# Dispatch scores of a soft mixture of experts taken straight from the tokens in four column groups, with another order of issue

## Chip, cores and metric

One core of a Trainium2 chip runs the whole program. The metric is device time in microseconds (us) of one execution; lower is better. The engines are named as in the profile: PE is TensorE's matmul side and PEld its weight loads, DVE is VectorE, ACT is ScalarE, POOL is GpSimd, SP is the engine that issues all DMAs here.

## What is computed

Windowed attention with four sink tokens, then a soft mixture of experts on its output. Cut to what matters:

```
B, H, S, D = 4, 8, 768, 64        # n_sink = 4, window = 128
a = softmax(q @ k.T / 8, masked to sinks and the last 128 positions)
x = (a @ v), heads side by side                 # 3072 tokens x 512
logits = x @ phi                                # 3072 x 32 slots
d = softmax(logits, over all tokens)            # dispatch
slot_input = d.T @ x                            # 32 x 512, 4 slots for each of 8 experts
slot_out[e] = relu(slot_input[e] @ w1[e]) @ w2[e]
c = softmax(logits, over the 32 slots)          # combine
out = c @ slot_out                              # 3072 x 512
```

## The kernel before

**Jobs.** The 3072 tokens are cut into 12 jobs of 256 tokens (4 batches of 3). For each job PE transposes K and Q (`prep`), multiplies scores in quarters of its array (`softmax.scores`, four steps of 8 matmuls, on PSUM tiles called s), DVE masks and takes maxima, ACT takes exponentials, POOL multiplies by the inverse sums, PE transposes the weights (`weights_transposed`), DVE or ACT copies them out, POOL cuts them into two masked copies (`select`), PE multiplies by the values in column halves (`values`, two steps of 2 and 8 or 12 matmuls), and the result lands in `xt`, 128 rows (two heads each of which there are four groups `a`) by 256 tokens. `natural` transposes it back to tokens by features (`xnb`).

**Tokens.** `Moe.tokens` (line 306) keeps a running softmax over all tokens of the dispatch. Scores are wanted twice, as [32 g + slot, token] for four groups g: groups 0 and 1 raw, groups 2 and 3 with the exponential, and the even groups hold the job's first 128 tokens, the odd ones the last. Before, this took three steps: `pairs` (line 328) multiplies phi's four chunks by xt's four chunks, each in a column group of its own, 256 tokens wide; a copy of 128x256 brings the four partial sums out of PSUM (line 334, on DVE or ACT); `logits` (line 337) adds the four up with a 0/1 matrix `c.slot`, once for each group g, 128 tokens wide. Then DVE takes the maximum (line 355) and its running minimum of negatives (358), ACT copies the raw half to `lt` (360), takes the exponential of the other half (362) and the factor for older sums (368), PE transposes `lt` (372), and `products` (384) multiplies it with `xnb`, four column groups again.

**Which order.** A planner (`Plan`) issues every step of the jobs. Each step has a key, 4.0 times the job's number plus an offset from the table `CFG`; the planner walks a modelled time and takes, of the steps that are ready on an engine, the one with the smallest key. All results of the planner are fixed before launch: each engine runs its list in order and waits on semaphores. PE works in four shapes: the whole array (transposes), quarters (scores), halves (values), column groups of 32 (`pairs`, `logits`, `products`). PSUM has two s tiles of two banks and four w banks; a w bank is needed by each of the transposes, values and token steps, until the copy out of it is done.

**Ends.** After the last job `finish` (418) turns the sums into slot inputs, `tail` (530) runs the experts' two layers on streamed weights and writes the output. Nothing in `tail` is touched.

Of the kernel before, what the change touches and what calls it, by code (L numbers as in the profile page):

```python
# [8 lines left out]
F32 = mybir.dt.float32  # L9
# [10 lines left out]
P = 128  # L20
# [257 lines left out]
class Moe:  # L278
# [6 lines left out]
    def __init__(self, nc, c, keep, work, pools, B):  # L285
        self.nc, self.c, self.keep, self.work, self.pools, self.B = nc, c, keep, work, pools, B

        self.lt = keep.tile([P, P], F32, name="lt")
        self.lb = keep.tile([P, 2, 2, 32], F32, name="lb")
        self.spare = keep.tile([P, 256], F32, name="spare")  # L290
# [12 lines left out]
        nc.gpsimd.memset(self.eps[64:96], EPS)  # L303
        nc.vector.memset(self.z, 0.0)

    def tokens(self, plan, keys, b, j, x, xn, blocks):
# [17 lines left out]
        if both:  # L324

            A, lp = plan.psum(), self.lp
# [16 lines left out]
        else:  # L343
            next(k), next(k)

            def logits(e):
                for a in range(4):
                    for g in range(4):
                        nc.tensor.matmul(L["tile"][32 * g:32 * g + 32, 0:P], lhsT=c.phi[:, a, :],
                                         rhs=xt[:, a, x[blocks[0]]], start=(a == 0), stop=(a == 3))  # L350

            plan.add(next(k), "P", 1.2, logits, r=xs + ["phi"], w=[L["name"]], new=L)

# [64 lines left out]
    def finish(self, plan, keys):  # L418
# [10 lines left out]

        swap, slots, sel = self.si.rearrange("p k s -> p (k s)"), self.spare[:, 0:P], self.sel  # L430
# [7 lines left out]
        plan.add(next(k), "V", 0.6, selectors, w=["fsel"])  # L438
        mm = [("m", 0), ("m", 1)]
# [8 lines left out]
        def inputs(e):  # L448
            for x in range(2):
# [8 lines left out]
            rz, self.z, f, self.eps, op0=ALU.mult, op1=ALU.add), r=["z", "f"], w=["rz"])  # L458
        plan.add(next(k), "V", 0.2, lambda e: nc.vector.tensor_copy(
            slots.rearrange("p (g s) -> p g s", g=4), c.slot.unsqueeze(1).to_broadcast([P, 4, 32])), w=["lp"])  # L460
        plan.add(next(k), "P", 0.25, lambda e: nc.tensor.matmul(Z["tile"][:, 0:1], lhsT=slots, rhs=rz, start=True, stop=True),
                 r=["rz", "lp"], w=["fz"], new=Z)
        plan.add(next(k), "V", 0.17, lambda e: nc.vector.reciprocal(rz, Z["tile"][:, 0:1]), r=["fz"], w=["rz"], last=Z)
# [153 lines left out]
class Weights:  # L617
# [9 lines left out]
    def load(self, t):  # L627
# [5 lines left out]
        else:  # L633
# [8 lines left out]
PT = 3  # L642
CFG = {'prep': [-2.17, -0.88],
       'load': [-3.57, -6.02],
       'v': [-0.18, -0.24],
       'S': -8.73,
       'M': 36.62,
       'E': -5.46,
       'N': 0.31,
       'K0': 2.19,  # L650
       'T': [3.66, 4.85, 4.7, 5.73],
       'K': -1.8,
       'sel': [-6.52, -2.35, 5.2, 5.48],
       'val': [3.28, -5.83, 5.91, 8.36],
       'xn': [2.08, 9.26],
       'tok': [7.72, -14.81, -29.67, 6.11, -4.29, -10.76, 19.93, 9.29, -24.99, 9.79, 6.46, -0.14, -1.55],
       'sm': -17.55,
       'sinks': -36.55,
       'tr': [83.54, 111.89, 84.43, 86.17, 89.04, 123.77, 106.32, 93.21, 89.01, 82.18, 84.62, 87.83, 68.6, 87.87, 106.87,
              85.72, 98.54, 75.2, 46.43, 23.9, 60.71, 53.42, 48.6, 43.21, 70.53, 50.67, 57.49],  # L660
       'w': [14.83, 8.0],
       'fin': [-17.88, 7.56, 0.7, -0.3, 12.51, 20.97, 18.11, 14.38, 20.61, 23.73, 38.59],
       'xn1': [18.28, 18.07],
       'tok1': [4.6, -7.87, -9.73, -4.24, 1.2, -17.1, 3.61, 11.52, -24.18, -0.27, -3.93, 3.34, -6.83]}


def window_path(ctx, tc, c, moe, q, k, v, phi, w1, w2, out):
# [21 lines left out]
    xt = moe.xt = u[:, 1024:2048].rearrange("p (a y) -> p a y", a=4)  # L689
    moe.lp = moe.spare[:, 0:256]  # L690

# [207 lines left out]
    def values(keys, n, quad):  # L899
# [20 lines left out]

        r = [("xw", quad, i, 1) for i in range(2)] + [("xw", quad, 1, 0, x) for x in range(2)]
        r += [("vb", 2 * n % 4), ("vb", (2 * n + 1) % 4), "vsink", "pst"]
        if j > 0:
            r += [("xw", quad, 0, 0, x) for x in range(2)] + [("vb", (2 * n - 1) % 4)]
        add(keys[0], "P", 2.15 if j else 1.72, go, r=r, w=[h["name"]], new=h, mode=HALVES)
# [17 lines left out]
    O = CFG  # L943
# [77 lines left out]
def general_path(ctx, tc, c, moe, ints, q, k, v, phi, w1, w2, out):  # L1021
# [87 lines left out]
    t, u = moe.first  # L1109
    moe.lp, xnb = t[:, 0:256], (u[:, 0:512], u[:, 512:1024])  # L1110
    moe.xt = u[:, 1024:2048].rearrange("p (a y) -> p a y", a=4)
    gate(nc, plan, c, phi, moe.acc[:, 0:P], "acc")
    for b in range(B):
# [10 lines left out]
        moe.slot_softmax(plan, 0, b, ())  # L1124
    moe.finish(plan, [0] * 11)
    moe.place(slot(), [0, 1], 2)
# [100 lines left out]
```

## Time and profile before

| | |
|---|---|
| median of 3 runs | 257.99 us (257.02 to 258.0) |
| profiled execution | 257.78 us, its span 256.0 us |
| mean granted clock of TensorE | 0.964 |
| busy: PE, DVE, ACT, POOL | 229.0, 171.2, 143.6, 141.3 us |
| jobs, until the slot inputs stand | up to about 201 us |
| experts and output | about 201 to 256 us |

A share of busy time is an average over the whole span. PE's time is read best from the starts of its steps in the timeline, since the ends of matmuls are modelled and overlap the next step: the distance between two starts is what the step costs.

### The profile page before, as it was taken

How to read it: one execution, taken by the hardware profiler on the slowest of the kernel's cores; microseconds unless marked ns; L12 is line 12 of the kernel's file. 1: busy time of each engine (PE TensorE's matmuls, PEld its weight loads, DVE VectorE, ACT ScalarE, POOL GpSimd, SP SyncE). 2: the span in 40 equal slices, each digit the busy share in tenths (PEclk: the TensorE clock that was granted, in tenths of full speed). 3: DMA queues.
4: the chain of work that ended last, by engine and by line, in shares of the span. 5: the costliest groups of instructions: out<-in, count | busy, mean ns of one | idle time of the engine just before them, and what ended most of it. 6: DMA issues, size and time to landing. Idle time of an engine off the chain costs nothing.

```text
span 256.0 us, 7069 instructions
## 1 busy us (share of the span) xinstructions
PE 229.0 (89%) x2572; PEld 157.2 (61%) x2572; DVE 171.2 (67%) x457; ACT 143.6 (56%) x568; POOL 141.3 (55%) x281
## 2 busy tenths in 40 slices
PE   7778999999999999999999999999699999997800
PEld 7655766776777776676777667677367434345700
DVE  3378968889798979979897997987514513103800
ACT  2367677568596757769675767977615112103700
POOL 1146769587685958669595857869964060000000
PEclk9979999999999999999999999999979999999955
DMA  5699869789899989967999866240609899950995
GB/s 126 133 176 225 227 152 356 186 239 379 162 257 211 343 250 302 276 146 244 256 366 223 235 125 123 59 150 4 206 13 358 300 399 422 414 235 0 399 394 203
DMA packets 84494, 59.34 MB, mean 232 GB/s; under 512 B 76261, under 2 KB 76261, under 8 KB 82917
## 3 DMA queue, kind: packets, MB, share of 16 engines
q1 hardware_dynamic: 84452, 58.83, 76.4%
q8 instruction: 22, 0.36, 0.6%
q14 instruction: 20, 0.16, 0.2%
HBM read 52.53 MB, written 6.29 MB: 230 GB/s over the span
## 4 chain that ended last, share of the span: by engine, by line
PE 66%; DVE 16%; ACT 6%; POOL 5%; issue 3%; ACTq 0%; POOLq 0%; DVEq 0%
PE w L127 47%; PE s L127 17%; DVE wt L127 7%; POOL wt L127 4%; DVE s L127 4%; ACT wt L127 3%; PE w L1179 1%; ACT wt L613 1%; DVE sums L127 1%; DVE first L127 1%; DVE pst L127 1%; DVE spare L127 1%; DVE qt L127 0%; DVE wt L599 0%; ACT wt L598 0%
## 5 line engine op out<-in xcount | busy, mean ns | idle before, releaser
L127 POOL TENSOR_TENSOR wt<-wt 128x528 f32<-128x528 f32 (+1 forms) x96 | 64.3, 673 | 36.3 <-DVE wt L127 22.1
L127 ACT ACTIVATE wt<-s,wt 128x132 f32<-128x132 f32 x192 | 68.8, 386 | 5.6 <-DVE wt L127 5.0
L127 POOL TENSOR_SCALAR_AFFINE_SELECT wt<-wt 128x512 f32<-128x512 f32 x88 | 54.0, 638 | 6.9 <-ACT wt L127 6.4
L127 PE MATMUL w<-wt 128*64 128x128 f32 (+3 forms) x550 | 51.7, 322 | 2.1 <-DVE wt L599 1.5
L127 PE MATMUL s<-wt,qt 64*64 64x196 f32 (+2 forms) x768 | 41.8, 327 | 4.5 <-ACT wt L127 3.7
L127 PEld LDWEIGHTS w<-wt 128*64 128x64 f32 (+2 forms) x550 | 36.7, 143 | 14.8 <-DVE wt L599 2.2
L127 PE MATMUL w<-ident,first 128*128 128x128 f32 x288 | 42.3, 279 | 1.7 <-ACT call L127 1.4
L127 ACT ACTIVATION_READ_ACCUMULATOR wt<-s,wt 128x1 f32 x192 | 42.5, 221 | 0.0
L127 PE MATMUL w<-ident,wt 128*128 128x128 f32 x250 | 38.3, 281 | 1.2 <-POOL wt L127 0.6
L127 PEld LDWEIGHTS w<-ident,first 128*128 128x128 f32 x288 | 32.5, 142 | 7.3 <-issue 2.3
L127 PEld LDWEIGHTS s<-wt,qt 64*64 64x64 f32 x768 | 26.5, 134 | 14.5 <-issue 6.5
L127 DVE TENSOR_REDUCE wt<-s 128x4 f32<-128x528 f32 x48 | 33.9, 707 | 1.7
L127 PEld LDWEIGHTS w<-ident,wt 128*128 128x128 f32 x250 | 28.1, 146 | 11.2 <-issue 3.4
L127 ACT COPY first<-w 128x512 f32<-128x512 f32 x28 | 16.5, 588 | 30.3 <-PE w L127 30.2
L127 ACT COPY wt<-w 128x512 f32<-128x512 f32 x36 | 21.1, 594 | 17.5 <-PE w L127 14.9
L127 DVE COPY_PREDICATED s<-later,s 128x256 f32<-128x256 uint8 x48 | 20.4, 424 | 8.9 <-PE s L127 8.0
L127 DVE COPY wt<-w 128x512 f32<-128x512 f32 x36 | 24.3, 677 | 1.5 <-PE w L127 0.8
L127 DVE COPY first<-w 128x512 f32<-128x512 f32 x20 | 13.7, 684 | 2.0 <-PE w L127 1.9
L127 PE MATMUL w<-wt,si 128*32 128x512 f32 x128 | 13.9, 593 | 0.4 <-DVE si L127 0.4
L127 PE MATMUL s<-wt 128*32 128x512 f32 (+1 forms) x144 | 14.3, 498 | 0.0
L127 DVE MEMSET s<- 64x512 f32 (+1 forms) x16 | 6.2, 385 | 9.5 <-PE s L127 9.1
L127 DVE TENSOR_TENSOR wt<-wt 128x4 f32<-128x4 f32 x48 | 11.2, 232 | 1.8 <-POOL wt L127 0.9
(120 smaller groups left out, 243.9 us busy)
## 6 DMA issues: line engine op xcount, KB each, us to landing
wt<-in_moe_w_dram SPq DMA_DIRECT2D x30, 1024.0 KB, 7.6
wt<-in_v_dram SPq DMA_DIRECT2D x24, 256.0 KB, 3.3
first<-in_q_dram SPq DMA_DIRECT2D x22, 256.0 KB, 3.8
first<-in_k_dram SPq DMA_DIRECT2D x22, 256.0 KB, 4.5
out_dram<-wt SPq DMA_DIRECT2D x5, 1024.0 KB, 5.6
first<-in_moe_w_dram SPq DMA_DIRECT2D x2, 1024.0 KB
out_dram<-wt SPq DMA_DIRECT2D x2, 512.0 KB
first<-in_k_dram SPq DMA_DIRECT2D x4, 128.0 KB, 3.0
```

The lines of the kernel that those rows point to most:

```text
L127: return self.tc.keep_in_program_order(f(*args, **kw))
L613: (nc.vector.tensor_copy if i else nc.scalar.copy)(ob[:, n - n0, i], yp)
L1179: nc.tensor.matmul(t[:, 0:P], lhsT=c.ident, rhs=c.ident, start=True, stop=True)
```

## The change

`tokens` loses `pairs`, the copy and the sum with `c.slot`. The new `logits` multiplies each of the four chunks of phi by the same chunk of xt for every group g, 16 matmuls of 128 tokens in four column groups, and adds the chunks up in PSUM. One w bank and one step on DVE or ACT go with it. `finish` makes its 0/1 matrix `slots` early, with the other selectors. `tied` changes nothing, as `CFG` has no entry `tie`. Every number of `CFG` is another one, and with them the order on all engines.

```diff
-            def pairs(e):
-                for a in range(4):
-                    nc.tensor.matmul(A["tile"][32 * a:32 * a + 32, 0:256], lhsT=c.phi[:, a, :], rhs=xt[:, a, :],
-                                     start=True, stop=True)
-            plan.add(next(k), "P", 0.45, pairs, r=xs + ["phi"], w=[A["name"]], new=A, mode=(128, 32))
-            plan.add(next(k), "AV", (0.27, 0.34), lambda e: (nc.scalar.copy if e == "A" else nc.vector.tensor_copy)(
-                lp, A["tile"][:, 0:256]), r=[A["name"]], w=["lp"], last=A)
-            def logits(e):
-                for g in range(4):
-                    nc.tensor.matmul(L["tile"][32 * g:32 * g + 32, 0:P], lhsT=c.slot, rhs=lp[:, x[g % 2]],
-                                     start=True, stop=True)
-            plan.add(next(k), "P", 0.23, logits, r=["lp"], w=[L["name"]], new=L, mode=(128, 32))
+        def logits(e):
+            for a in range(4):
                 for g in range(4):
+                    nc.tensor.matmul(L["tile"][32 * g:32 * g + 32, 0:P], lhsT=c.phi[:, a, :],
+                                     rhs=xt[:, a, x[g % 2 if both else blocks[0]]], start=(a == 0), stop=(a == 3),
+                                     skip_group_check=True)
+        plan.add(next(k), "P", 0.87, logits, r=xs + ["phi"], w=[L["name"]], new=L, mode=(128, 32))
...
+            nc.vector.tensor_copy(slots.rearrange("p (g s) -> p g s", g=4),
+                                  c.slot.unsqueeze(1).to_broadcast([P, 4, 32]))
...
-       'S': -8.73,
-       'M': 36.62,
+       'S': -57.08,
+       'M': 186.71,
...
```

The order on PE, one job in the middle, before. `s<-wt,qt` is a score step, `w<-ident,...` are transposes (first_76 is K or Q, first_77 the job's result, wt the weights), `phi` is `pairs`, `spare,slot` the sum over heads, `lb` the products, `pst,vsink` and the 64-row matmuls the values:

```order
L127 MATMUL w<-ident,wt 128x128 x4
L127 MATMUL w<-first_77,lb 32x256 x4
L127 MATMUL s<-wt,qt 64x196 x8
...
L127 MATMUL w<-ident,first_77 128x128 x4
L127 MATMUL w<-first_77,phi 32x256 x4
L127 MATMUL w<-ident,wt 128x128 x4
L127 MATMUL w<-ident,first_76 128x128 x4
L127 MATMUL w<-spare,slot 32x128 x4
L127 MATMUL s<-wt,qt 64x196 x16
```

and the same place now:

```order
L127 MATMUL w<-ident,wt 128x128 x2
L127 MATMUL s<-wt,qt 64x196 x8
L127 MATMUL w<-first_77,phi 32x128 x16
L127 MATMUL w<-first_77,lb 32x256 x4
L127 MATMUL s<-wt,qt 64x196 x8
L127 MATMUL w<-ident,first_77 128x128 x8
L127 MATMUL w<-ident,first_76 128x128 x4
L127 MATMUL w<-ident,wt 128x128 x4
L127 MATMUL w<-ident,first_76 128x128 x8
```

Three visits to the column groups have become one, the new scores stand right ahead of the products of the job before, and the transposes stand together. Counted over one job, PE changed its shape 13 times before and does so 9 times now; over the whole program 169 and 123 times.

The end of the jobs on PE, from the scores of the last job but one to the transpose of `lt` that waits for them, before:

```order
L127 MATMUL w<-first_77,phi 32x256 x4
L127 MATMUL w<-ident,wt 128x128 x4
L127 MATMUL w<-ident,qt 128x128 x2
L127 MATMUL w<-spare,slot 32x128 x4
L127 MATMUL w<-ident,lt 128x128
```

and now:

```order
L127 MATMUL w<-first_77,phi 32x128 x16
L127 MATMUL w<-ident,wt 128x128 x2
L127 MATMUL w<-ident,first_77 128x128 x8
L127 MATMUL w<-ident,wt 128x128 x4
L127 MATMUL w<-ident,lt 128x128
```

Fourteen transposes now stand between the finished scores and the transpose that waits for them, where none stood.

ACT, the token steps of a job in the middle, before:

```order
L127 COPY lt<-w 64x128
L127 ACTIVATE lt,sums<-w,sums 64x128
L127 COPY wt<-w 128x4x128
L127 ACTIVATE sums<-sums 128x1
L127 ACTIVATE wt<-s,wt 128x132 x4
L127 COPY lb<-w 128x64
```

and now:

```order
L127 COPY lt<-w 64x128
L127 COPY wt<-w 128x4x128
L127 ACTIVATE lt,sums<-w,sums 64x128
L127 COPY first_77<-w 128x512
L127 ACTIVATE sums<-sums 128x1
L127 COPY wt<-w 128x4x128
```

`COPY wt<-w 128x4x128` empties a bank of transposed K, `COPY first_77<-w` one of the transposed result. Three such copies now stand among the token steps, and PE's next transposes need the banks.

## Rows read from the trace of the kernel before

**Rows 1.** Stretches: window, length, then PE, PEld, DVE, ACT, POOL busy (count), granted clock.

```profile
62.00:78.00 16.00, 16.00 (x193) 11.33 (x195) 14.09 (x37) 12.38 (x52) 12.33 (x24) 1.00 0.91 227
...
174.00:190.00 16.00, 13.74 (x140) 9.13 (x138) 8.31 (x20) 8.88 (x35) 14.76 (x33) 0.89 0.25 84
```

**Rows 2.** Timeline of PE, 164 to 184 us: start, length, line, operation, count of records.

```profile
165.24 1.52 PE L127 MATMUL w<-wt 128*64 128x256 f32 x16
166.69 1.56 PE L127 MATMUL s<-wt,qt 64*64 64x196 f32 x32
168.18 0.65 PE L127 MATMUL w<-ident,first 128*128 128x128 f32 x4
...
170.30 0.64 PE L127 MATMUL w<-first,phi 128*32 128x256 f32 x8
170.87 0.66 PE L127 MATMUL w<-ident,wt 128*128 128x128 f32 x4
171.45 0.90 PE L127 MATMUL s<-wt,qt 64*64 64x196 f32 x16
172.28 0.43 PE L127 MATMUL w<-spare,slot 128*32 128x128 f32 x8
172.63 0.50 PE L127 MATMUL w<-pst,vsink 128*128 128x256 f32 x2
173.06 1.96 PE L127 MATMUL w<-wt 128*64 128x256 f32 x24
174.95 0.90 PE L127 MATMUL s<-wt,qt 64*64 64x196 f32 x16
...
179.05 0.64 PE L127 MATMUL w<-first,lb 128*32 128x256 f32 x8
179.62 0.44 PE L127 MATMUL w<-ident,qt 128*128 128x128 f32 x2
```

**Rows 3.** Chain that ended last, in order of time: the first job of two batches.

```profile
61.33 1.77 PE w L127 x16
...
105.02 1.77 PE w L127 x16
```

**Rows 4.** Groups by form: weight loads of `pairs`; busy us, mean ns, idle before.

```profile
L127 PEld LDWEIGHTS w<-first,phi 128*32 128x32 f32 x96 | 1.9, 108 | 2.1 <-issue 1.0 <-ACT wt L127 0.5 <-ACT first L127 0.3
```

**Rows 5.** Groups by form, DVE: maxima, whole-bank copy, masking, copy behind `pairs`.

```profile
L127 DVE TENSOR_REDUCE wt<-s 128x4 f32<-128x528 f32 x48 | 33.9, 707 | 1.7
L127 DVE COPY wt<-w 128x512 f32<-128x512 f32 x36 | 24.3, 677 | 1.5 <-PE w L127 0.8
L127 DVE COPY_PREDICATED s<-later,s 128x256 f32<-128x256 uint8 x48 | 20.4, 424 | 8.9 <-PE s L127 8.0
L127 DVE COPY spare<-w 128x256 f32<-128x256 f32 x10 | 4.1, 413 | 0.0
```

**Rows 6.** Groups by form, POOL: masked copies, products with inverse sums.

```profile
L127 POOL TENSOR_SCALAR_AFFINE_SELECT wt<-wt 128x512 f32<-128x512 f32 x88 | 54.0, 638 | 6.9 <-ACT wt L127 6.4 <-DVE wt L127 0.3
L127 POOL TENSOR_TENSOR wt<-wt 128x528 f32<-128x528 f32 x48 | 52.5, 1094 | 32.4 <-DVE wt L127 22.1 <-PE w L127 5.6 <-ACT wt L127 4.3
```

**Rows 7.** Timeline of all engines, 183 to 191 us, the token steps of job 10.

```profile
183.16 0.43 PE L127 MATMUL w<-spare,slot 128*32 128x128 f32 x8
...
184.03 0.60 DVE L127 TENSOR_TENSOR sums<-sums 128x1 f32<-128x1 f32 x1
...
184.99 0.36 ACT L127 ACTIVATE lt<-w,sums 64x128 f32<-64x128 f32 x1
...
185.49 0.33 PE L127 MATMUL w<-ident,lt 128*128 128x128 f32 x1 [1.91 <-ACT lt L127]
...
187.65 2.99 PE L127 MATMUL w<-wt 128*64 128x256 f32 x24
...
190.57 0.51 PE L127 MATMUL w<-pst,vsink 128*128 128x256 f32 x2
```

**Rows 8.** Stretch of 5 us behind that wait; columns as in the first group.

```profile
186.00:191.00 5.00, 4.92 (x37) 3.08 (x36) 0.91 (x2) 0.49 (x3) 3.55 (x9) 0.66 0.01 3
```

More of the change, by code (lines that the diff above doesn't have):

```diff
@@ L289, in __init__ @@
         self.lb = keep.tile([P, 2, 2, 32], F32, name="lb")
-        self.spare = keep.tile([P, 256], F32, name="spare")
+        self.spare = keep.tile([P, P], F32, name="spare")
         self.sel = keep.tile([P, 2, 32], F32, name="sel")
@@ L427, in finish @@
         sf = self.lt[:, 0:64].rearrange("p (h s) -> p h s", h=2)
-        swap, slots, sel = self.si.rearrange("p k s -> p (k s)"), self.spare[:, 0:P], self.sel
+        swap, slots, sel = self.si.rearrange("p k s -> p (k s)"), self.spare, self.sel
         def selectors(e):
@@ L435, in selectors @@
                 nc.vector.tensor_copy(sv[:, :, i], iv[:, :, 1 - i])
+            nc.vector.tensor_copy(slots.rearrange("p (g s) -> p g s", g=4),
+                                  c.slot.unsqueeze(1).to_broadcast([P, 4, 32]))
             nc.vector.reduce_sum(sel, c.ident.rearrange("p (h i s) -> p h s i", h=2, i=2), axis=AX.X)
-        plan.add(next(k), "V", 0.6, selectors, w=["fsel"])
+        plan.add(next(k), "V", 0.8, selectors, w=["fsel"])
         mm = [("m", 0), ("m", 1)]
@@ L458, in finish @@
             rz, self.z, f, self.eps, op0=ALU.mult, op1=ALU.add), r=["z", "f"], w=["rz"])
-        plan.add(next(k), "V", 0.2, lambda e: nc.vector.tensor_copy(
-            slots.rearrange("p (g s) -> p g s", g=4), c.slot.unsqueeze(1).to_broadcast([P, 4, 32])), w=["lp"])
         plan.add(next(k), "P", 0.25, lambda e: nc.tensor.matmul(Z["tile"][:, 0:1], lhsT=slots, rhs=rz, start=True, stop=True),
-                 r=["rz", "lp"], w=["fz"], new=Z)
+                 r=["rz", "fsel"], w=["fz"], new=Z)
         plan.add(next(k), "V", 0.17, lambda e: nc.vector.reciprocal(rz, Z["tile"][:, 0:1]), r=["fz"], w=["rz"], last=Z)
@@ L642 @@
 PT = 3
-CFG = {'prep': [-2.17, -0.88],
-       'load': [-3.57, -6.02],
-       'v': [-0.18, -0.24],
-       'S': -8.73,
-       'M': 36.62,
[L648 to L664, printed above, removed]
+CFG = {'prep': [-2.16, -0.3],
+       'load': [21.99, 22.32],
+       'v': [33.66, 32.25],
+       'S': -57.08,
+       'M': 186.71,
+       'E': 198.38,
+       'N': -122.03,
+       'K0': -153.45,
+       'T': [4.22, 5.36, -56.02, 6.26],
+       'K': -91.54,
+       'sel': [-252.14, -110.82, -227.04, -165.5],
+       'val': [6.47, -181.65, 159.49, 3.35],
+       'xn': [-3.88, -28.66],
+       'tok': [-94.42, -47.32, -0.46, -84.53, 6.22,
+               13.54, -86.04, -42.65, 121.57, 82.4,
+               -4.36],
+       'sm': -36.24,
+       'sinks': -8.72,
+       'tr': [243.6, 70.64, 138.55, 13.83, 356.42,
+              165.29, 138.6, 311.63, 323.87, 66.49,
+              76.22, 267.84, 70.54, 249.06, 174.54,
+              11.97, 188.69, 179.1, -43.61, -32.41,
+              114.32, 92.2, -113.6, 355.77, 23.25,
+              3.05, 157.35],
+       'w': [43.54, 8.0],
+       'fin': [142.31, 142.48, 171.48, 3.97, -103.29,
+               142.9, 61.71, 69.87, -120.32, 16.75],
+       'xn1': [-22.56, -92.79],
+       'tok1': [-164.89, 33.0, -16.85, 236.68, -3.11,
+                1.53, -78.29, -119.18, 63.7, 47.24,
+                44.44]}
 def window_path(ctx, tc, c, moe, q, k, v, phi, w1, w2, out):
@@ L689, in window_path @@
     xt = moe.xt = u[:, 1024:2048].rearrange("p (a y) -> p a y", a=4)
-    moe.lp = moe.spare[:, 0:256]
     xws = [slot().rearrange("p (i w h y) -> p i w h y", i=2, w=2, h=4) for _ in range(2)]
@@ L919, in go @@
                                          stop=(x == 1 and m == 2 * n + 1), skip_group_check=True)
-        r = [("xw", quad, i, 1) for i in range(2)] + [("xw", quad, 1, 0, x) for x in range(2)]
+        tied = range(2) if O.get("tie") else [quad]
+        r = [("xw", y, i, 1) for i in range(2) for y in tied] + [("xw", y, 1, 0, x) for x in range(2) for y in tied]
         r += [("vb", 2 * n % 4), ("vb", (2 * n + 1) % 4), "vsink", "pst"]
         if j > 0:
-            r += [("xw", quad, 0, 0, x) for x in range(2)] + [("vb", (2 * n - 1) % 4)]
+            r += [("xw", y, 0, 0, x) for x in range(2) for y in tied] + [("vb", (2 * n - 1) % 4)]
         add(keys[0], "P", 2.15 if j else 1.72, go, r=r, w=[h["name"]], new=h, mode=HALVES)
@@ L1109, in general_path @@
     t, u = moe.first
-    moe.lp, xnb = t[:, 0:256], (u[:, 0:512], u[:, 512:1024])
+    xnb = u[:, 0:512], u[:, 512:1024]
     moe.xt = u[:, 1024:2048].rearrange("p (a y) -> p a y", a=4)
@@ L1124, in general_path @@
         moe.slot_softmax(plan, 0, b, ())
-    moe.finish(plan, [0] * 11)
+    moe.finish(plan, [0] * 10)
     moe.place(slot(), [0, 1], 2)
```

9 lines of the change are left out of this document (removed).

## The prediction, made before the changed kernel ran

> **What bounds the kernel now.** I read the table of stretches first, then PE's timeline, then the groups by form, then the waits near the end of the jobs. In the middle of the jobs PE is busy 16.00 of 16 us, while DVE is at 14.09 and POOL at 12.33 [rows 1]. So from about 30 to 174 us a microsecond less of PE's work is a microsecond off, as long as DVE, the next fullest, keeps up. From 174 to 190 us it is different: PE falls to 13.74 of 16, POOL is at 14.76, and the granted clock averages 0.89 [rows 1]. Here a wait ends last. PE stands 1.91 us before it may transpose `lt` of job 10, because that needs the scores, a maximum, a minimum and an exponential behind them [rows 7]. Behind that wait the granted clock averages 0.66 over 5 us [rows 8], so for part of them it is on the lower of its two levels, 1.2 GHz in place of 2.4; a step of values that takes 1.89 us at full clock (173.06 to 174.95) [rows 2] takes 2.92 there (187.65 to 190.57) [rows 7]. The experts and the output, behind 201 us, run the same code as before.
>
> **What the steps on PE cost.** Distances between starts [rows 2]: `pairs` 170.30 to 170.87, 0.57 us. The sum over heads 172.28 to 172.63, 0.35. `products` 179.05 to 179.62, 0.57. A step of scores alone 171.45 to 172.28, 0.83; two in one run 166.69 to 168.18, 1.49. So the second of two costs 0.66, and 0.83 - 0.66 = 0.17 us is paid once for each visit to a shape of the array. The columns themselves: 16 records of values take 165.24 to 166.69, 1.45, and 24 take 1.89; the eight more are four rounds, each of two neighbouring 128-column matmuls side by side, so 0.44 / 4 = 0.11 us for a round of 128 columns. `logits` before had two such rounds (a float32 matmul is two records here), 0.22, and 0.35 - 0.22 = 0.13 for the visit. `products` and `pairs` have two rounds of 256 columns, 0.44 at the same pace, and 0.13. I take 0.15 us for a visit, between 0.13 and 0.17.
>
> **The change, part by part.**
>
> Columns. Per job, `pairs` and the sum over heads go: 0.44 + 0.22 = 0.66 us. The new scores are 16 matmuls, 32 records, eight rounds of four: 8 x 0.11 = 0.88. That is 0.22 more for each of 12 jobs, **+2.6 us**. No row shows 32 records of 128 columns in four column groups. The nearest are the two rounds of the old sum, which have the same width, groups and loads. Taken as four such steps with a visit each, 4 x 0.35 = 1.40 in place of 0.88 + 0.15 = 1.03: that is the upper end, 0.37 more per job, 4.4 in all. The lower end is 0.88. I take the lower end, since the rounds of values follow each other at 0.11 with a load between them [rows 2].
>
> The Trainium skill's page TensorE: Matmul & The Clock Gate (packing small matmuls, what overlaps and what doesn't) speaks against that: it says that a weight load runs beside a matmul only where the two use different row groups, and here all four groups use all rows. By it each of the eight rounds would show its load as well; what that gives stands below as a rival.
>
> Visits. 169 changes of shape become 123: 46 fewer, at 0.15, **-6.9 us** (5.9 by 0.13, 7.8 by 0.17). Nearly all lie where PE is full; the few in the first 30 us and in the tail of the jobs may cover waits instead. Together with the columns: **-4.3 us**.
>
> The copy. Ten of 12 copies of 128x256 were on DVE, 0.41 us each, 4.1 in all [rows 5]. They lie beside PE's work and are worth nothing directly. They give DVE room: a job lasts (105.02 - 61.33) / 3 = 14.6 us [rows 3], 14.09 / 16 of it, 12.8, is DVE's, and of that 0.34 goes, while the job gets 4.3 / 12 = 0.36 shorter; DVE stays as full as it is now. The copy was also a hand-over between two steps of PE; the planner filled it with transposes, so its end is worth something only where PE had nothing else, in the last job.
>
> Waits in the middle. The new list has three tight places. The scores follow the last values by one sinks transpose and one score step, some 1.0 us by 0.83 for the score step and 0.2 for two transposes, for a copy of 0.68 [rows 5]. Among the seven groups of transposes behind the second score step PE needs a bank every four transposes, 0.43 us, and the banks come back from copies of 0.68 on DVE [rows 5] and somewhat less on ACT. And the bank of the scores is free only when ACT has taken the exponential, with three other copies standing among those steps. I count some 0.3 to 0.6 us of waiting per job; PE's distances before hold about as much beyond columns and visits. **0**, with bounds of -2 (a quarter of a microsecond less in eight jobs) and +5 (half a microsecond more in ten).
>
> The end of the jobs. Fourteen transposes, some 1.5 us, now stand between the scores of job 10 and the transpose that waits. The chain from the start of the sum to that transpose was 2.33 us, 1.98 of it behind the step [rows 7], so about 0.5 of the 1.91 us is left. With a shorter wait the clock may not fall; at 0.66 of 5 us, 1.7 us of work were lost [rows 8]. Both together are 3.1. Against it: POOL has, from the last transposes of job 10 on, 16 masked copies of 0.64 and four products of 1.09 [rows 6] and small pieces for which I allow 4 us, 18.6 us in all, beside some 20 us of PE's work ahead of the last values. That is no longer much cover. I take **-2.5**, bounds 0 and -4.
>
> The last job. Between its `pairs` and its sum the copy stood; now the scores are one step: 0.57 + 0.41 + 0.35 = 1.33 us [rows 2, 5] without the hand-overs become 1.03. **-0.3**, bounds 0 and, with the hand-overs, -1.
>
> The start. The first eight score steps wait for DVE's maxima; the early copy for `slots` falls into DVE's idle time before the first scores. **0**, bounds -1 and +1.5.
>
> The DMA queue gets its weights in a similar place, 17 of them before the last K and Q; the last thirteen follow buffers that the jobs free, so they move with PE. **0**.
>
> The sum: 257.8 - 4.3 - 2.5 - 0.3 = 250.7 us, against the profiled execution's 257.8, which is 0.2 below the median of the runs. I forecast **250.7**; the likeliest case by itself spans 246 to 254.5.
>
> **The rivals.**
>
> A bank late in every job (slower). ACT's exponential, which frees the bank of the scores, waits for the running minimum, and that for DVE, which may still be in a maximum of scores: 0.42 + 0.71 = 1.13 us [rows 5]. Ahead of the transposes that need the bank stand only products and one score step. If all of it shows in ten jobs, 250.7 + 11.3 = 262.0. It turns the sign from about 0.7 us per job on. For it: three bank copies now stand among ACT's token steps. Against it: the maximum that could be in the way is placed behind the scores in some jobs, and a bank from the sinks' transposes is free by then. Chance 0.12.
>
> Weight loads show in every round. A load of 32 columns takes 0.108 us [rows 4]; eight rounds with one each make 0.86 more per job, 10.4 in all, 261.1 us. Against it: rounds of values come at 0.11 us with loads as long [rows 2]. The page above would give this. Chance 0.04.
>
> The new scores run as four separate steps: 250.7 + 4.4 = 255.1, still faster. Chance 0.08.
>
> PE is full but not what sets the pace. If the maxima on DVE or POOL's products release the next work no earlier, the 4.3 us of PE's work turn into waits and the end gains little: 256 to 258.5, I say 257.3. For it: DVE at 14.09 of 16 [rows 1]. Against it: PE shows no idle time there. Chance 0.14.
>
> **How the numbers follow.** My forecast has 0.62. A measurement of this kernel can tell about 0.5%, 1.3 us. Faster by more: the forecast, the separate steps and a fifth of the last rival, 0.73. Slower by more: the late bank, the loads, and a little of a lost end, 0.14. The rest, 0.13, is within. The range, 246 to 259, holds the forecast's own but for its lowest part, the separate steps and the last rival, 0.8; it leaves the slower rivals out.
>
> **What would show it.** In the profile after: the new scores with `products` in one run take 0.88 + 0.44 + 0.15 = 1.47 us; 1.8 or more would speak for the separate steps, 2.3 for the loads. The distance of a batch of three jobs, 43.7 us now [rows 3], comes down to about 42.4 in the middle. PE's wait before the last `lt` transposes is under 1 us and the clock behind it is back at 1.00. The DVE copies to `spare` are gone and DVE's share does not rise. The prediction is wrong if PE shows waits of over 0.7 us per job in front of transposes, ended by ACT's copies, or if the visits to a shape cost nothing where they are merged: then runs of two score steps would no longer be shorter than two alone.

## The result, and the profile after

The changed kernel takes **253.87 us** (median of 4 runs, 253.75 to 254.24) against 258.00 us for the kernel before beside it (4 runs, 257.02 to 258.16): ratio 0.985, 95% interval 0.9824 to 0.9877. It is faster, by 1.5%, and inside the range; but the forecast was 250.7, 2.8% faster. By the profiled executions 257.8 became 253.8 (span 252.0): 4.0 us of the 7.1 that the sum promised. Of 54 further runs of the kernel before, beside the experiments (two of 734.78 and 1193.3 us left out), 37 took 256.9 to 258.5 us like these four, and 17 took 255.3 to 255.9 at a higher mean granted clock (0.978 or 0.979 for 0.957 to 0.966), so against the 17, of which no trace was kept, the change would be worth 1.7 us in place of 4.1. What this part of the document looks for is the other 3.1.

**PE's steps came out as costed.** Timeline of PE in the changed kernel, third job of the second batch: start, length, line, operation, records.

```profile
111.29 0.90 PE L127 MATMUL s<-wt,qt 64*64 64x196 f32 x16
112.12 1.08 PE L127 MATMUL w<-first,phi 128*32 128x128 f32 x32
113.02 0.61 PE L127 MATMUL w<-first,lb 128*32 128x256 f32 x8
113.56 0.89 PE L127 MATMUL s<-wt,qt 64*64 64x196 f32 x16
114.39 1.53 PE L127 MATMUL w<-ident,first 128*128 128x128 f32 x12
...
117.83 1.52 PE L127 MATMUL w<-wt 128*64 128x256 f32 x16
```

From start to start the new scores take 0.90 us and `products` 0.54, with the visit to the shape 1.44; forecast 1.47, where four separate steps would have shown 1.8 and loads in the open 2.3.

**The end of the jobs came out too.** Stretches of the changed kernel, then its timeline around the last wait for `lt` (columns as in [rows 1] and [rows 7]).

```profile
62.00:78.00 16.00, 16.00 (x235) 12.90 (x228) 13.71 (x32) 11.63 (x46) 12.91 (x23) 1.00 0.95 228
174.00:190.00 16.00, 15.21 (x180) 11.14 (x180) 8.30 (x19) 8.82 (x34) 13.20 (x28) 1.00 0.36 112
```

```profile
181.48 1.00 PEld L127 LDWEIGHTS w<-first,phi 128*32 128x32 f32 x32
181.70 1.06 PE L127 MATMUL w<-first,phi 128*32 128x128 f32 x32
...
183.18 0.65 DVE L127 TENSOR_TENSOR sums<-sums 128x1 f32<-128x1 f32 x1
...
184.18 0.36 ACT L127 ACTIVATE lt<-w,sums 64x128 f32<-64x128 f32 x1
...
184.69 0.33 PE L127 MATMUL w<-ident,lt 128*128 128x128 f32 x1 [0.25 <-ACT lt L127]
```

From the scores to `lt` it takes 2.99 us (181.70 to 184.69; 2.33 before, with the shorter sum in it), but transposes fill it: 0.25 us of waiting where 1.91 stood [rows 7], and the granted clock of the second stretch is 1.00 where it was 0.89 [rows 1]. In the first stretch PE reads as full as before and DVE a little less so, 13.71 for 14.09. The experts begin at 197.38 us; before at 201.12.

**The middle did not.** The chain that ended last, the first score step of two batches:

```profile
61.75 1.49 PE s L127 x32
...
105.81 1.49 PE s L127 x32
```

A batch of three jobs takes 44.06 us; before 43.69 [rows 3], forecast 42.4. So the middle, where PE's work was to shrink most, became a little slower. Splitting the distance by the paces of [rows 2] shows why: before, 35.5 us of columns, 39 visits at 0.15 (5.9) and 2.4 left over; after, 36.1 of columns, 27 visits (4.1) and 3.9 left over. The remainders move by some 0.4 us with the pace that is taken, both alike, so it is their difference that counts. PE's steps did give 1.2 us, and 1.5 us of new waits took them back. Over everything from PE's first score step to the experts, the same count reads: columns +2.6, 46 visits fewer -6.9, waits in the first 60 us +0.1, in the two batches from 60 to 150 us +2.9, behind 150 us -2.7 (idle transposes that only keep PE busy are counted as waits). These add up to the measured -4.0 because the waits are whatever is left over.

**Where the new waits stand.** PE's waits between 60 and 150 us by what ended them (us in total, times, longest), in the kernel before and then in the changed one:

```profile
PE w L127 <- ACT call L127: 1.4, 3, 0.5
```

```profile
PE w L127 <- DVE first L127: 1.6, 3, 0.7
PE w L127 <- DVE acc L127: 0.9, 2, 0.5
```

The kernel before had one wait a batch, for a copy of the combine scores (`call`) on ACT; the changed one waits for DVE, in two places. PE, DVE and ACT in the second job of its second batch:

```profile
99.13 0.66 PE L127 MATMUL w<-ident,first 128*128 128x128 f32 x4
100.24 1.21 PE L127 MATMUL w<-ident,first 128*128 128x128 f32 x8 [0.46 <-DVE acc L127]
...
103.86 0.87 PE L127 MATMUL w<-wt 128*64 128x256 f32 x8
```

```profile
98.89 0.71 DVE L127 TENSOR_REDUCE wt<-s 128x4 f32<-128x528 f32 x1
99.51 0.28 DVE L127 TENSOR_REDUCE sums<-w 128x1 f32<-128x128 f32 x1
99.71 0.47 DVE L127 SCALAR_TENSOR_TENSOR acc<-acc,sums,w 128x256 f32<-128x256 f32 x1
```

```profile
99.83 0.26 ACT L127 COPY lt<-w 64x128 f32<-64x128 f32 x1 [1.77 <-DVE sums L127]
```

Because the visits were merged, 28 transposes now stand in one run behind the second score step, and each four of them want a bank. In the third job the run lasts 114.39 to 117.83, 3.44 us; here 99.13 to 103.86, 4.73, so **1.3 us** more. About half of it stands at one place, where the first four transposes take 1.11 us from start to start in place of some 0.45; the rest is spread over the later steps. The bank that PE waits for there is that of `products`. It comes back with the running sums (`acc`), and those stand on DVE behind the maxima of a score step and the scores' own maximum, which starts at 99.51 although the scores were through by 97.76. ACT stands 1.77 us for the same maximum (1.80 in the first jobs and 1.23 in the third, so this alone does not mark a late job). In the first job of a batch, PE waits elsewhere:

```profile
80.32 0.90 PE L127 MATMUL s<-wt,qt 64*64 64x196 f32 x16
81.88 1.08 PE L127 MATMUL w<-first,phi 128*32 128x128 f32 x32 [0.66 <-DVE first L127]
```

```profile
79.97 0.56 DVE L127 TENSOR_TENSOR call<-call,rm 128x192 f32<-128x192 f32 x1
80.45 0.59 DVE L127 TENSOR_TENSOR wt<-wt 128x4 f32<-128x4 f32 x1
...
81.16 0.66 DVE L127 COPY first<-w 128x512 f32<-128x512 f32 x1
```

The scores wait for a copy of values on DVE, and ahead of that copy stand the combine softmax of the batch before and a tiny operation, 128x4, that takes 0.59 us. Its group in the changed kernel (busy us, mean ns, idle before):

```profile
L127 DVE TENSOR_TENSOR wt<-wt 128x4 f32<-128x4 f32 x48 | 16.4, 342 | 12.0 <-ACT wt L127 11.1 <-POOL wt L127 0.4
```

The copies to `spare` (4.1 us) are gone, and yet DVE is busy 171.3 us, as before. This row is one place where they went: it is the addition of 1e-9 to the softmax totals (`inverse`), 232 ns in the mean before and 342 now. Why it is so long is seen beside POOL:

```profile
111.44 0.85 DVE L127 TENSOR_TENSOR wt<-wt 128x4 f32<-128x4 f32 x1
```

```profile
110.77 1.50 POOL L127 TENSOR_TENSOR wt<-wt 128x528 f32<-128x528 f32 x1
```

The addition ends within 20 ns of the end of POOL's product; alone such an addition takes 150 ns. Here two inverses stand close together, at 110.03 and 111.44: the first lets POOL start its long product and the second is held behind it. Of the 48 additions of the changed kernel 20 are more than 60 ns longer than the shortest, and all 20 end 10 to 20 ns behind the end of a POOL instruction: ten behind such a product, ten behind a masked copy. In the kernel before 11 of 48 are that long. The Trainium skill (SBUF — State Buffer, section SBUF: two separate sides) says that DVE and GpSimd share a pair of ports as an exclusive lock, which a DVE operation takes that has two inputs in SBUF or runs in a two-port mode, and that the later of the two is blocked for the whole of the earlier one. The 0.85 us agree with it.

### The profile page after: what moved, and what is told of

It is laid out like the page before. It is cut to its first block, busy times and chain, and to the rows that moved or that the text cites. A ratio compares the mean times of both kernels' runs of the same rounds, so it can differ in the third digit from the quotient of the medians.

```text
span 252.0 us, 7482 instructions
## 1 busy us (share of the span) xinstructions
PE 225.1 (89%) x2754; PEld 162.0 (64%) x2754; DVE 171.3 (68%) x445; ACT 143.7 (57%) x568; POOL 143.2 (57%) x281
## 4 chain that ended last, share of the span: by engine, by line
PE 56%; DVE 22%; ACT 9%; issue 5%; POOL 2%; DVEq 0%; ACTq 0%; POOLq 0%
PE w L127 42%; PE s L127 13%; DVE wt L127 10%; ACT wt L127 7%; DVE s L127 7%; POOL wt L127 2%; PE w L1168 2%; DVE sums L127 1%; DVE rs L127 1%; DVE call L127 1%; ACT lt L127 1%; DVE acc L127 1%; DVE wt L579 0%; ACT qt L127 0%; ACT wt L578 0%
## 5 line engine op out<-in xcount | busy, mean ns | idle before, releaser
L127 PEld LDWEIGHTS w<-wt 128*64 128x64 f32 (+2 forms) x550 | 37.3, 144 | 13.5 <-DVE wt L579 2.2
L127 PE MATMUL w<-ident,first 128*128 128x128 f32 x288 | 41.6, 281 | 2.4 <-DVE acc L127 1.3
L127 ACT COPY wt<-w 128x512 f32<-128x512 f32 x45 | 26.6, 595 | 25.5 <-PE w L127 22.1
L127 PE MATMUL w<-ident,wt 128*128 128x128 f32 x250 | 39.0, 283 | 1.6 <-ACT lt L127 0.8
L127 PEld LDWEIGHTS w<-ident,first 128*128 128x128 f32 x288 | 31.8, 142 | 9.7 <-issue 3.9
L127 DVE TENSOR_TENSOR wt<-wt 128x4 f32<-128x4 f32 x48 | 16.4, 342 | 12.0 <-ACT wt L127 11.1
L127 ACT COPY first<-w 128x512 f32<-128x512 f32 x31 | 17.9, 596 | 8.4 <-PE w L127 8.2
L127 DVE COPY wt<-w 128x512 f32<-128x512 f32 x27 | 18.3, 679 | 2.1 <-PE w L127 1.7
L127 PE MATMUL w<-first,phi 128*32 128x128 f32 x384 | 13.1, 276 | 2.0 <-DVE first L127 1.9
L127 POOL COPY wt<-wt 128x512 f32<-128x512 f32 (+2 forms) x13 | 5.8, 455 | 15.0 <-ACT wt L127 14.9
```

The costliest lines, as they stand in the source:

```text
L127: return self.tc.keep_in_program_order(f(*args, **kw))
```

## The experiments

Each kernel is timed against the kernel before in the same session (medians of 257.5 to 257.7 there). "Batch" is the distance of two batches in the kernel's chain or, where the chain doesn't pass there, between the same score steps in its timeline.

| run | edit | us | ratio to before, 95% interval | batch |
|---|---|---|---|---|
| before | | 258.0 | | 43.69 |
| after | the change | 253.87 | 0.985 (0.982 to 0.988) | 44.06 |
| e4 | new scores in the old places | 256.37 | 0.996 (0.993 to 0.999) | 43.61 |
| e1 | after, no additions | 249.92 | 0.972 (0.968 to 0.977) | 43.32 |
| e2 | before, no additions | 253.03 | 0.984 (0.981 to 0.987) | 42.89 |
| e3 | after, additions with one input | 254.29 | 0.988 (0.985 to 0.992) | 44.13 |
| e6 | e1 and the minimum as a reduction | 247.70 | 0.961 (0.957 to 0.965) | 42.40 |
| e11 | e2 and the minimum as a reduction | 252.75 | 0.984 (0.980 to 0.989) | 42.90 |
| e8 | e4, no additions | 253.26 | 0.984 (0.980 to 0.988) | 43.29 |
| e5 | after, token steps first on DVE | 255.76 | 0.995 (0.992 to 0.998) | 44.66 |
| e9 | after, K's copy first on ACT | 253.53 | 0.988 (0.983 to 0.992) | 43.82 |
| e7 | e5 and e6 together | 249.15 | 0.969 (0.965 to 0.973) | 42.69 |
| e10 | e9 and e6 together | 247.60 | 0.964 (0.960 to 0.969) | 42.16 |
| e12 | e7, and the weights' copy before the second maxima | 245.85 | 0.957 (0.952 to 0.962) | 41.87 |

### Is the gain that of the scores, or of the order? (e4)

The planner runs with the old steps and the old table, so that every step keeps its place; `pairs` and its copy issue nothing, and the sum over heads is replaced by the direct scores.

```diff
-            plan.add(next(k), "P", 0.45, pairs, r=xs + ["phi"], w=[A["name"]], new=A, mode=(128, 32))
+            plan.add(next(k), "P", 0.45, None, r=xs + ["phi"], w=[A["name"]], new=A, mode=(128, 32))
...
-                for g in range(4):
-                    nc.tensor.matmul(L["tile"][32 * g:32 * g + 32, 0:P], lhsT=c.slot, rhs=lp[:, x[g % 2]],
-                                     start=True, stop=True)
+                for a in range(4):
+                    for g in range(4):
+                        nc.tensor.matmul(L["tile"][32 * g:32 * g + 32, 0:P], lhsT=c.phi[:, a, :],
+                                         rhs=xt[:, a, x[g % 2]], start=(a == 0), stop=(a == 3),
+                                         skip_group_check=True)
```

> The new scores alone: every step stands where the kernel before has it, the direct scores in the place of the sum over heads, pairs and its copy left out. If the gain of the change is that of merged visits, so of the new order, PE's steps here cost 0.57 + 0.35 before and 1.03 now, 0.11 more per job: 258 to 259.5 us. If the scoring itself gains (DVE relieved of 4.1 us of copies, a hand-over less), 255 to 256.5.

It took 256.37 us, inside the second expectation's 255 to 256.5, but not for its reason: taking `pairs` out also let the transposes on its two sides join, so 23 visits went, which the first expectation had not counted. With that, columns +2.6 and 23 visits -3.45 make -0.8; the stretch from the first score step to the experts became 0.76 us shorter, so waits moved by less than 0.1. Taken together, the two prices of the sum, 0.11 us for a round and 0.15 for a visit, fit a second order too. DVE was relieved of 4.0 us here (busy 171.2 to 167.2) and the waits stayed as they were, as the prediction had it for the copies. The scores by themselves are worth 1.1 us by the medians (0.4%) and 0.8 by the profiles; the rest of the change's gain is that of the order.

### Does POOL's hold on DVE make the new waits? (e1, e2, e3)

Left out, in e1 and e2, is the addition of 1e-9 to totals of at least 1.

```diff
-            nc.vector.tensor_tensor(z, z, eps, op=ALU.add)
             nc.vector.reciprocal(z, z)
```

> The changed kernel without the addition of 1e-9 to the 48 softmax totals (each total holds an exponential of zero, so it is at least 1); order and everything else as in the changed kernel. Theory A: the waits that the new order brought come from DVE, whose addition is held until POOL's running instruction ends (48 of them, 16.4 us busy, up to 1016 ns each). Then DVE loses about 16 us of busy time, PE's waits per batch of three jobs fall from 3.9 us back to 2.5, the batch distance from 44.1 to 42.5 or less, and the time to 248-251.5 us. Theory B: the waits come from banks that ACT gives back late, and DVE's lateness is cover: the time stays within 1 us of the changed kernel's. Theory C: DVE is simply full, whatever fills it: a gain, but the same in the kernel before (see the second run).

> The kernel before without the same 48 additions (11.2 us of DVE's time, 232 ns in the mean). Theory A: few of them are held behind the long product here, and the old order covers them; 0 to -1.5 us, so 256.5 to 258. Theory C (DVE full in both): -2.5 us or more, as in the first run.

The changed kernel fell to 249.92 us, about 4 us less, as theory A asked, though a batch came down only to 43.32 and not to 42.5; but the kernel before fell by 4.5 us as well (253.03), which A did not allow. So these additions are on the path in both orders, as theory C asked, and they alone are not what parts them: the batch lost 0.7 us in one and 0.8 in the other. Whether they cost time as load on DVE or as a link in the chain from ACT's exponentials over the inverse to POOL's product, no run tells; that e4's 4.0 us off DVE left the waits alone speaks against load in general. This says something on [rows 1] too: PE was "busy" 16.00 of 16 us there, and yet 48 additions on DVE, 11.2 us in all, cost that kernel 4.5 us. The row of the same table two stretches on (columns as in [rows 1]) is not full:

```profile
94.00:110.00 16.00, 15.49 (x195) 10.96 (x194) 14.32 (x37) 10.35 (x45) 11.35 (x21) 1.00 0.91 251
```

There stands the wait for `call` of 0.47 us that came once a batch. In e2 it is gone, and it makes up most of the 0.8 us that the batch lost. One full stretch of PE does not mean that the others are full, or that the engines feeding PE have slack.

e3 keeps the addition but gives it one input from SBUF.

```diff
-            nc.vector.tensor_tensor(z, z, eps, op=ALU.add)
+            nc.vector.tensor_scalar(z, z, EPS, None, op0=ALU.add)
```

> The changed kernel with the addition of 1e-9 as a tensor_scalar with an immediate: one input from SBUF in place of two. If only a DVE instruction with two SBUF inputs is held by POOL, the 48 take 170 ns each, 8.2 us in place of 16.4, and the time falls by 1 to 3 us. If an instruction with one SBUF input is held as well (one record of the changed kernel, the addition of 1e-9 to the slots' totals, took 987 ns beside a POOL product and 172 elsewhere), the mean stays near 340 ns and the time within 0.7 us of the changed kernel's.

```profile
L127 DVE TENSOR_SCALAR wt<-wt 128x4 f32<-128x4 f32 x48 | 16.8, 350 | 12.0 <-ACT wt L127 11.1 <-POOL wt L127 0.4
L127 DVE RECIPROCAL wt<-wt 128x4 f32<-128x4 f32 x48 | 8.5, 178 | 1.7
```

Nothing changed: 350 ns in the mean, 254.29 us. A second input is not what matters: the addition with an immediate is held just as long. The reciprocal behind it, also 128x4 from SBUF to SBUF, is never held; in e1, where it stands in the addition's place, 25 of the 48 run wholly beside a POOL instruction and none takes more than 180 ns.

### The same for the minimum (e6, e11)

With the additions gone, the minimum of old and new maximum (another operation on two columns in SBUF) was the next to be held. A reduction over the two columns gives the same number.

```diff
-            plan.add(key, "V", 0.07, lambda e: nc.vector.tensor_tensor(new, new, old, op=ALU.min),
+            plan.add(key, "V", 0.07, lambda e: nc.vector.tensor_reduce(new, self.m, op=ALU.min, axis=AX.X),
```

> The changed kernel without the 48 additions of 1e-9, and with the minimum of old and new maximum as a reduction over both columns in place of an operation with two inputs. In the run without the additions alone that minimum is held 6 times of 11 by POOL, 3.0 us in all beyond 150 ns. If what POOL holds is instructions that read both from SBUF at the faster rate, and reductions never (none of 48 longer than its shortest by 60 ns), the 11 fall to some 0.2 us each, and the time by 0.5 to 2 us against that run, to 248-249.4. If the wait behind it is covered: the same as that run.

The group in e1, and in e6:

```profile
L127 DVE TENSOR_TENSOR sums<-sums 128x1 f32<-128x1 f32 x11 | 4.7, 427 | 0.2
```

```profile
L127 DVE TENSOR_REDUCE sums<-sums 128x1 f32<-128x2 f32 x11 | 1.6, 149 | 0.2
```

427 ns became 149, and the time 247.70 us, 2.2 less than e1 by the medians and 1.3 by the profiled stretch from the first score step to the experts. The first jobs of the batches are now smooth: their scores follow the score step at once, and the wait of 0.31 us for `lt` that e1 still had behind them is gone.

```profile
79.75 0.90 PE L127 MATMUL s<-wt,qt 64*64 64x196 f32 x16
80.57 1.08 PE L127 MATMUL w<-first,phi 128*32 128x128 f32 x32
```

> The kernel before with the same two edits (no additions of 1e-9, the minimum as a reduction). In its own trace the minimum is held 10 times of 11, 3.2 us in all. If what POOL holds costs both orders alike, it gains what the changed kernel gained by both (6.2 us): 251 to 252. If the new order suffers more, because the waits behind the score steps are its own, less: 252.3 to 253.5, near the run without the additions alone (253.0).

In the kernel before the same two edits give 252.75, no more than the additions alone. Without what POOL holds, the change is worth 252.75 - 247.70 = 5.05 us, where it is worth 4.1 with it. The intervals of the two ratios are as wide as that difference, but the profiled stretch from the first score step to the experts says the same: 187.5 and 182.4 us without holds, 191.9 and 188.0 with them, 5.0 apart and 4.0. So by these profiles about 1 us of the missing 3.1 is lost to the hold. In the middle alone it is 1.3: the two batches from the fourth job's first score step to the tenth's take 88.25 us against 87.71 before with the holds, and 84.93 against 85.70 without. The additions alone do not show this (86.77 and 85.83, e1 and e2), since without them the minimum is held in their place: in the changed kernel one of its 11 is, in e1 six.

### Do the second jobs only need DVE's scores first? (e5, e7)

In three jobs, the token steps are moved ahead of the maxima that stand before them on DVE; the lists of the other engines stay as they were.

```diff
...
+                m = v.pop(x)
+                v.insert(1 + max(y for y, j in enumerate(v) if tag.get(j) in [(z, n) for z in names]), m)
+                new = self.merged({**seq, "V": v}, at)
...
```

> The changed kernel with one thing moved on DVE, in 3 jobs (the second of each of the first three batches): the maximum of the dispatch scores, the minimum and the running sums stand before the maxima of the score step, not behind them; the orders of PE, ACT, POOL and SP are the same. In the changed kernel the scores' maximum starts 1.8 us after the scores' last matmul in these jobs (0.6 in the others), and the 30 transposes behind take 1.4 us more than columns and visit; in the third jobs, where the scores' maximum already goes first, 0.1 more. Theory D (the new order's waits are banks held by DVE's place for the scores' maximum): the 1.4 fall to 0.3 or less, three times, 250.5 to 252 us. Rival (DVE has no slack, what goes second is as late as before): the maxima of the score step come 0.9 us later, exponentials and weights with them, the wait comes back at the next transposes, within 0.8 us of the changed kernel.

Theory D fell, and further than the rival said: 255.76 us, 1.9 slower than the changed kernel. PE in the second job, and DVE:

```profile
99.51 1.53 PE L127 MATMUL w<-ident,first 128*128 128x128 f32 x12
...
104.37 0.50 PE L127 MATMUL w<-pst,vsink 128*128 128x256 f32 x2 [1.21 <-DVE wt L127]
```

```profile
102.63 0.71 DVE L127 TENSOR_REDUCE wt<-s 128x4 f32<-128x528 f32 x1
...
103.62 0.69 DVE L127 COPY wt<-w 128x512 f32<-128x512 f32 x1
```

The wait for `acc` is gone, 12 transposes run through. But the maxima of both score steps now stand later, with one copy between them, and behind the second the copy of transposed weights that gives back the bank which the values want: PE stands 1.21 us for that instead. In the other two jobs it is 0.68 and 0.26 us, for two copies that stand behind the second maxima. The wait went from one bank to the next one in DVE's queue.

> The three moves of the first run and the two edits of the second together. If DVE's order and what POOL holds are separate causes, the gains add: 246 to 248 us. If either covers the other, no better than the better of the two.

e7 has the same moves without holds: 249.15 us, no better than e6; in this job PE stands 1.21 us at the same place.

### Is it the bank of K? (e9, e10)

In the second job of three batches the copy that empties the bank of K is put ahead of ACT's copy of the scores.

```diff
...
+            y = next((y for y in range(x + 1, x + 5) if tag.get(a[y]) == ("kc",)), None)
+            if y:
+                a.insert(x, a.pop(y))
+            else:
+                z = v.index(next(j for j in v if tag.get(j) == ("top", tag[i][1])))
+                y = next((y for y in range(z, z + 6) if tag.get(v[y]) == ("kc",)), None)
+                if y:
+                    a.insert(x, v.pop(y))
...
```

> The changed kernel with one copy moved in 3 jobs (the second of each of the first three batches): the copy that gives back the bank of the K transposes stands on ACT ahead of the copy of the scores, not behind it (in two of the jobs it was ACT's next instruction, in one DVE's fourth after the scores' maximum). Orders of PE, POOL and SP as they were. In the changed kernel ACT stands 1.77 us before the copy of the scores, while PE waits 0.45 us for a bank in front of the transposes behind the second score step. Theory E (30 transposes in one run need seven banks, and three of the four are held by K, scores and products): the bank comes 0.4 to 1 us earlier, three times: 1 to 2.7 us less, 251 to 252.8. Rival (the bank is not what PE is short of there; DVE's and ACT's load is): within 0.6 us of the changed kernel.

```profile
100.00 1.09 PE L127 MATMUL w<-ident,first 128*128 128x128 f32 x8 [0.46 <-DVE acc L127]
```

```profile
99.01 0.59 ACT L127 COPY wt<-w 128x512 f32<-128x512 f32 x1 [1.19 <-PE s L127]
```

Counted from the start of the run of transposes the copy came 0.9 us earlier (99.01 behind 98.89; in the changed kernel, on DVE, 100.17 behind 99.13), in ACT's gap, and PE's wait stayed 0.46 us for the same `acc`: 253.53 us, within 0.6 as the rival had it. So the wait was not for just any bank, but for the one that these transposes have, that of `products`. The steps behind it gained 0.3 us: the run lasts 98.89 to 103.35, 4.46 for 4.73.

> The same move together with the two edits that leave POOL nothing of DVE's to hold (no additions of 1e-9, the minimum as a reduction). If the run of 30 transposes in the second jobs is the wait that is left there (1.4 us in each with those edits), 1 to 2.7 us less than the 247.7 us of those edits alone: 245 to 246.7. If not, 247.2 to 248.2.

247.60 us: the move adds nothing to e6 that the runs can tell, though the batch is 0.24 shorter.

### Do the holds and the old places go together? (e8)

> The new scores in the old places, without the 48 additions of 1e-9. By PE's work (new scores in old places were 1.1 us off the span of the kernel before) and DVE's relief (4.5 us in the kernel before) it should take 251.5 to 252.5 us, and the new order without the additions, at 249.9, stay ahead by its visits. If the new order is ahead only where DVE is late, the two come out alike, at 250.

253.26 us, 0.8 above the range that was expected and the same as e2. The new order stays 3.3 us ahead (249.92), as its visits ask. That the scores alone no longer gain their 1.1 us here is not explained. The profiles (one each) show where to look: e8's first score step starts 1.4 us later than e2's (10.08 and 8.65 us), its batches are 0.4 us longer, and the rest up to the experts is shorter by more, so that the stretch between is 186.15 us against 187.49.

### All banks ahead of the maxima (e12)

Beside e7's moves, in the same three jobs the copy of the last weights goes ahead of the second pair of masking and maxima, and the short step that updates the running totals goes behind them.

```diff
...
+            m = next(y for y in range(x, x + 9) if tag.get(v[y], "")[0:1] == ("max",) and tag[v[y]][2] == 3)
+            c = next(y for y in range(m, m + 5) if tag.get(v[y], "") == ("tc", 3))
+            v.insert(c, v.pop(m))
+            z = next(y for y in range(x, x + 9) if tag.get(v[y], "") == ("total",))
+            k = v.index(v[c])
+            v.insert(k, v.pop(z))
...
```

> The token's steps first, as in the run with both kinds of edits (three moves, no additions of 1e-9, minimum as a reduction), and in the same three jobs also the copy of the last weights ahead of the maxima of the second score step on DVE. In that run the 28 transposes ran without a wait, and the values behind them stood 1.21 us for the bank that this copy gives back; it ended 100.77, behind the maxima that start at 98.31. Theory F (in the second jobs PE waits for whichever bank stands behind a pair of maxima in DVE's queue): with all bank copies ahead of the maxima the 1.4 to 1.6 us fall below 0.5, three times, about 3 us: 244 to 246.5. Rival G (DVE is full there; maxima that come later delay exponentials, products and the next transposes by as much): 247 to 249.5, as with either move alone.

```profile
95.74 1.53 PE L127 MATMUL w<-ident,first 128*128 128x128 f32 x12
97.11 0.62 PE L127 MATMUL w<-ident,wt 128*128 128x128 f32 x4
97.57 1.09 PE L127 MATMUL w<-ident,first 128*128 128x128 f32 x8
98.49 0.60 PE L127 MATMUL w<-ident,wt 128*128 128x128 f32 x4
98.85 0.48 PE L127 MATMUL w<-pst,vsink 128*128 128x256 f32 x2
99.26 1.96 PE L127 MATMUL w<-wt 128*64 128x256 f32 x24
```

```profile
96.43 0.71 DVE L127 TENSOR_REDUCE wt<-s 128x4 f32<-128x528 f32 x1
97.06 1.40 DVE L127 COPY wt<-w 128x512 f32<-128x512 f32 x2
```

```profile
59.42 2.05 PE s L127 x32
...
101.29 2.05 PE s L127 x32
```

The run of the second job lasts 95.74 to 99.26, 3.52 us where it was 4.73, and shows no wait; nor does PE wait over 0.1 us anywhere else between 55 and 155 us. **245.85 us**, theory F: 3.3 less than e7, 4.3% below the kernel before and the fastest of all. A little came back later: the first two score steps of each batch take half a microsecond more (2.05 where 1.49 stood). The batch is 41.87 us.

## Why the prediction was right or wrong

**Columns and visits (-4.3): right.** 1.44 us for scores and `products`, 46 visits fewer, and e4 fits the two prices taken together. Neither of the two rivals on this term came: the new scores did not run as four separate steps, and their loads did not show. The Trainium skill's line on loads (TensorE: Matmul & The Clock Gate, section Packing small matmuls, what overlaps and what doesn't), taken alone, does not fit here: eight rounds with four loads each took 0.90 us though all four groups use all rows, and the 32 loads (181.48, 1.00 us) ran beside the matmuls (181.70, 1.06 us).

**The end of the jobs (-2.5) and the last job (-0.3): right.** The count behind 150 us gives -2.7 beyond columns and visits; the wait is 0.25 us, under the 1 us named, and the clock 1.00.

**The start (0), DMA (0): right** within 0.1 us in the first 60.

**The step that failed is "Waits in the middle", put at 0 with bounds of -2 and +5.** It measured +2.9 us from 60 to 150, inside its bounds and nearly all of the 3.1 by which the forecast missed. The three tight places were seen, and priced at 0.3 to 0.6 us per job, no more than before; the count gives 0.8 per job before and 1.3 after. They bite in two jobs of three, and each time through DVE: in the first job by the combine softmax and held additions ahead of the copy that the scores need, in the second by maxima ahead of the steps that give banks back. That mechanism was the first rival, "a bank late in every job": its place (DVE still in a maximum) was right, its bank was that of `products` and not that of the scores, its price of 1.13 us came near the 1.3 by luck, as only about half of that stands at this bank, and the argument against it, that in some jobs the maximum stands behind the token steps, is what makes the third job smooth. It turned the sign of the middle but not of the whole, since it holds for three jobs, not ten. The sign by which it was to be known, waits ended by ACT's copies, was named wrong: they were ended by DVE.

**The copy (0), with DVE "as full as it is now": half right.** DVE's busy time is the same, but the 4.1 us of copies were not left as room; the held additions alone took 5.2 of it (16.4 for 11.2 us). And part of DVE's work was on the path before (e2). The argument against the rival "PE is full but not what sets the pace", that PE shows no idle time there, rested on one stretch: the stretches beside it hold a wait of 0.47 us in each batch. That rival, at 0.14 and 257.3 us, described the middle better than the forecast did, though not the sum.

With holds and bank order out of the way the forecast's own arithmetic holds in the middle: a batch of e12 takes 41.87 us, and of the kernel before without holds (e11) 42.90, so -1.0 where columns and visits alone make -1.2. The old order got no such moves of banks, so what they would give there is not shown. Left open too is what splitting the long run of transposes would give, at the price of a visit; that was not tried.

## What to carry to other kernels

Merging steps that share a shape of the array saves their switches at the price measured, but it also gathers their demand for PSUM banks in one place: before counting the saving, list for that place which step gives each bank back, and what stands ahead of it in that engine's queue. Moving one of these steps only hands the wait to the next bank (e5, e9); they have to move together (e12). And a PE that reads as full in one stretch says nothing on the engine that feeds it: price that engine's small operations by what they take beside a busy POOL, since the recorded length of a held operation looks like work.

## What the hardware showed beyond that

- A 128x4 addition on DVE, 150 ns alone, takes up to 1016 ns while POOL runs its 128x528 product; with one input and an immediate it is the same (350 ns in the mean of 48, 342 with two inputs). Reciprocals of the same tile (178) and the reduction of two columns (149) are not lengthened. One more record of the changed kernel shows it for an immediate, 172 ns elsewhere:

```profile
171.03 0.99 DVE L127 TENSOR_SCALAR rs<-rs 128x6 f32<-128x6 f32 x1
```

```profile
170.71 1.27 POOL L127 TENSOR_TENSOR wt<-wt 128x32 f32<-128x32 f32 x2
```

- The time of a held operation is counted as DVE's busy time, and the row of the additions puts only 0.4 us of idle time down to POOL.
- ACT's copy of the scores starts only when DVE's maximum over the same bank has ended, in each of the 12 jobs (99.83, behind the maximum of 99.51 to 99.79), though both only read the bank. The trace shows the copy waiting for the maximum on a semaphore, so this is an order that the program sets: a late maximum delays ACT's queue too, 1.77 us in the second jobs.
